# A dilated gated convolution on one core: four buffers for chunks and sums, loads issued earlier, and new places for the side work

## The chip, the cores and the metric

The kernel runs on one core of a Trainium2 chip. The core has a matrix engine (TensorE, PE in the profile; its weight loads are PEld), a vector engine (VectorE, DVE), an engine for activations and copies (ScalarE, ACT), a general engine (GpSimd, POOL) and an engine that here only issues DMAs (SyncE, SP). On-chip data lie in SBUF, results of matmuls in PSUM, inputs and outputs in device memory. The metric is the device time of one execution, in microseconds (us).

## The reference

The input `x` has 2 sequences of 16000 steps with 256 channels, `w` holds three taps of 256 x 512, `w_o` is 256 x 256, all in bf16. With a dilation of 2 and causal padding:

```
h[t] = x[t] @ w[0] + x[t-2] @ w[1] + x[t-4] @ w[2]     # steps before the first are 0
f, g = h[..., :256], h[..., 256:]
out = (tanh(f) * sigmoid(g)) @ w_o
```

So each step needs three products of depth 256 and width 512, a gate, and one product of depth 256 and width 256.

## The kernel before

**Rows, chunks, groups.** Four consecutive steps of a sequence form one row, so a sequence has 4000 rows. A row's steps are the four phases j of a tile `xt`, which a transposing DMA fills with channels on the partitions. A *plain group* is up to 256 rows (1024 steps). A *chunk* is what one load brings, usually two groups (`load_chunk`, L135). Plain groups don't multiply three taps: from xc, yp (the two phase pairs, one of them a row earlier) DVE makes the difference `m` (`pre_m`, L316) and the sum `p` (`pre_p`, L322), POOL makes the differences `d` (`pre_d`, L328), and four products with sums of the taps' weights (`products`, L345) replace six. For each group `oi` runs over the four output blocks of 128 channels.

**p in two ways.** For the first groups DVE computes `p`. For chunks from `P_DMA` on it is a tile `ps`: a second transposing DMA loads half of it (`load_sums`, L151), and a DMA issued by POOL adds the other half in place (`add_sums`, L159), at a slot set by `ACC_LAG`.

**Wide groups.** Four groups of each sequence are taken with eight steps to a row. A wide group (`load_wide`, L210) gets its operands `qa`, `qb`, `qd` by POOL (`wide_part`, L219, six parts), `qp` by DVE for the first and POOL for the others (`wide_sum`, L244) and `qm` by DVE (`wide_diff`, L254). Its output blocks take 14 matmuls of 256 columns each instead of eight of 512. They need further sums of the weights, made in twelve steps of two halves (`weight_step`, L614; places in `W_AT`, engine in `W_ENG`), and the first wide group's parts at the places of `P_AT`, its sum and difference at `SUM_AT` and `DIFF_AT`.

**Order.** The program is written in one order, and each engine keeps it. The list `slots` (L544) holds 104 plain slots (group, oi) and 32 wide ones, placed by `SPACING`: so many plain slots, then a wide one. The loop at L645 handles slot k: the first products of slot k, the second products of slot k-1 (which need DVE's `combine` of slot k-1, L390), at most one output piece (`out_mm`, L448; none at slots in `HOLD`, two in `TWICE`), DVE's combine, and then side work: gates (`gate`, L424), `pre_m`, weight steps, POOL's parts, accumulations, ACT's activations, loads. A piece's result goes from PSUM to `osb` in the next slot, by ACT or in some cases by DVE (`EVICT_DVE`), and SP stores two pieces at a time. `osb` has four buffers.

**POOL behind DVE.** `after` (L308) makes a POOL operation wait for DVE's last operation on SBUF operands in its slot, so that POOL reads SBUF while DVE's sums read PSUM.

**Loads.** SP issues all chunk, sum and wide loads and nearly all stores, in order. Chunk tiles `xt` and sums `ps` have three buffers each, wide tiles `xq` two. A chunk is loaded in the last slot of a group when the next group lies in a chunk two before it (L762). Wide group n + 2 is loaded in the last slot (oi = 3) of wide group n (L711).

Of the kernel before, what the change touches and what calls it, by code (L numbers as in the profile page):

```python
# [9 lines left out]
ALU = mybir.AluOpType  # L10
# [3 lines left out]
def kernel(  # L14
# [19 lines left out]
    nc = tc.nc  # L34
    bf16 = mybir.dt.bfloat16
    f32 = mybir.dt.float32
    B, T, D = x.shape
    K, _, D2 = w.shape
    P = 128
    assert K == 3 and D % P == 0 and D2 == 2 * D and T % 64 == 0  # L40
    CT = D // P
    NT = D // P
    RH = 16
    RG = 256
# [4 lines left out]
    LAST = ((128,), (128, 128))  # L49
    N_DIRECT = 4  # L50
    N_WIDE = (4, 4)
    SPACING = (31, 1, 3, 1, 4, 2, 2, 2, 3, 1, 2, 2, 2, 1, 1, 1, 2, 1, 1, 2, 2, 1, 2, 1, 2, 1, 1, 2, 2, 1, 1, 2,)
    W_ENG = (0, 0, 0, 0, 0, 0, 0, 1, 0, 0, 0, 0)
    W_AT = (7, 7, 11, 14, 14, 14, 17, 17, 19, 19, 22, 25, 26, 27, 29, 29, 29, 30, 30, 30, 33, 34, 36, 36)
    P_AT = (9, 10, 10, 11, 12, 13, 14, 15, 16, 16, 17, 19, 20, 20, 21, 22, 24, 24, 25, 25, 26, 27, 29, 29)
    SUM_AT, DIFF_AT = 21, 25
    HOLD = (23,)
    TWICE = (113,)
    COPIES = 0
    EVICT_DVE = ()  # L60
    SUM_POOL = True
    SHORT_LAST = True
    GATE2 = False
    P_DMA = 4
    ACC_LAG = (6, 6, 6, 6, 7, 9, 13, 7, 6, 6, 6, 11, 9, 7, 10, 8, 13, 14, 8, 10)
    Q_PARTS = ((0, 1), ("s", 2), (3, 4), (5,))
    SPLIT_PROJ = 1
    W_STEP = 2
# [10 lines left out]
    groups, chunks, wides = [], [], []  # L79
    starts = [0] * B  # L80

    def add_groups(b, rs, cuts=()):
        cuts, i = list(cuts), 0
        while i < len(rs):
            n = cuts.pop(0) if cuts else 2
            part = rs[i:i + n]
            chunks.append((b, starts[b], sum(part), len(groups), len(part)))
            for r in part:
                col = starts[b] - chunks[-1][1]
                groups.append(dict(wide=False, b=b, r0=starts[b], R=r, chunk=len(chunks) - 1, col=col))  # L90
                starts[b] += r
            i += n

    ends = []
    for b in range(B):
        wide = N_WIDE[min(b, 1)]
# [11 lines left out]
    XW = max(c[2] for c in chunks)  # L108

    consts = ctx.enter_context(tc.tile_pool(name="consts", bufs=1))  # L110
    xt_pool = ctx.enter_context(tc.tile_pool(name="xt", bufs=3))
    d_pool = ctx.enter_context(tc.tile_pool(name="dd", bufs=3))
    p_pool = ctx.enter_context(tc.tile_pool(name="pp", bufs=3))
    ps_pool = ctx.enter_context(tc.tile_pool(name="ps", bufs=3))
    m_pool = ctx.enter_context(tc.tile_pool(name="mm", bufs=3))
    ss_pool = ctx.enter_context(tc.tile_pool(name="ss", bufs=3))
    xq_pool = ctx.enter_context(tc.tile_pool(name="xq", bufs=2))
# [4 lines left out]
    osb_pool = ctx.enter_context(tc.tile_pool(name="osb", bufs=4))  # L122
# [10 lines left out]
    xts = {}  # L133

    def load_chunk(c):  # L135
        b, r0, rc, _, _ = chunks[c]
        xt = xt_pool.tile([P, 4, CT, RH + XW], bf16, name="xt")
        xts[c] = xt
        if r0 == 0:
            nc.gpsimd.memset(xt[:, :, :, RH - 1:RH], 0.0)  # L140
        if c == 0:
            return
        lo = 0 if r0 == 0 else RH
        nc.sync.dma_start_transpose(
            out=xt[:, :, :, RH - lo:RH + rc].rearrange("p j ct r -> p (j ct) r"),
            in_=x[b, 4 * (r0 - lo):4 * (r0 + rc), :].rearrange("(r j) c -> r (j c)", j=4),
        )

    def load_sums(c):  # L151
        b, r0, rc, _, _ = chunks[c]
        sums[c] = ps_pool.tile([P, 2, CT, XW], bf16, name="ps")
        nc.sync.dma_start_transpose(
            out=sums[c][:, :, :, :rc].rearrange("p j ct r -> p (j ct) r"),
            in_=x[b, 4 * r0:4 * (r0 + rc), :].rearrange("(r j) c -> r (j c)", j=4)[:, :2 * D],
        )

    def add_sums(c):  # L159
        rc = chunks[c][2]  # L160
        nc.gpsimd.dma_start(
            out=sums[c][:, :, :, :rc], in_=xts[c][:, 2:4, :, RH - 1:RH - 1 + rc], accum_op=ALU.add,
        )
        added.add(c)

    sums, added = {}, set()
# [1 line left out]
    nc.vector.memset(warm[:], 0.0)  # L168
    w_taps = [consts.tile([P, CT, D2], bf16, name=f"w{k}_sb") for k in range(K)]
    wo_sb = consts.tile([P, NT, D], bf16)  # L170
    xn = consts.tile([P, 4, D], bf16, name="xn")
    w_in = [w[k].rearrange("(ct c) d -> c ct d", c=P) for k in range(K)]
    nc.sync.dma_start(out=xn[:], in_=x[0, 0:4 * P, :].rearrange("(r j) c -> r j c", j=4))
    for k in (TAPS[0], TAPS[2]):
# [6 lines left out]
    for c in range(2):  # L181
        load_chunk(c)
    load_chunk(2)
    loaded = 3

    wd0_sb = consts.tile([P, CT, D2], bf16)
    wd2_sb = consts.tile([P, CT, D2], bf16)
    ws_sb = consts.tile([P, CT, D2], f32)
    wf_sb = consts.tile([P, CT, D2], f32)
    wu_sb = consts.tile([P, CT, D2], bf16)  # L190
    wt_sb = consts.tile([P, CT, D2], bf16)
    wp_sb = consts.tile([P, CT, D2], bf16)
# [129 lines left out]
    def pre_p(g):  # L322
        xp, yp, xc, yc = views(g)
        G = groups[g]
        G["p"] = p_pool.tile([P, 2, CT, RG], bf16, name="pp")
        return nc.vector.tensor_tensor(out=G["p"][:, :, :, :G["R"]], in0=xc, in1=yp, op=ALU.add)

    def pre_d(g, part, eng, behind=None):  # L328
        xp, yp, xc, yc = views(g)
# [9 lines left out]
        return ins  # L339

    def sum_view(G, ct):
        assert G["chunk"] in added
        return sums[G["chunk"]][:, :, ct, G["col"]:G["col"] + G["R"]]

    def products(k, which):  # L345
        G, oi = at(k)
        o = O_ORDER[oi]
        osl = slice(o * P, (o + 1) * P)
        R = G["R"]
        N = 2 * R  # L350
        if which in (1, 2):
            G["ab"[which - 1], oi] = (ps_a, ps_b)[which - 1].tile([P, 2 * RG], f32, name="ab"[which - 1])
        wmat, mv, bank, first = {
            2: (wm_sb, lambda ct: G["m"][:, :, ct, :R], "b", True),
            1: (wp_sb, lambda ct: sum_view(G, ct) if G["chunk"] >= P_DMA else G["p"][:, :, ct, :R], "a", True),
            3: (wd0_sb, lambda ct: G["d"][:, 2:4, ct, :R], "b", False),
            0: (wd2_sb, lambda ct: G["d"][:, 0:2, ct, :R], "a", False),
        }[which]
        for ct in range(CT):
            nc.tensor.matmul(  # L360
                G[bank, oi][:, :N], lhsT=wmat[:, ct, osl], rhs=mv(ct),
                start=first and ct == 0, stop=ct == CT - 1, skip_group_check=True,
            )
# [178 lines left out]
    NG = len(groups)  # L542
# [3 lines left out]
    for i, (_, g, oi) in enumerate(plain):  # L546
        slots.append(plain[i])
        since += 1
        full = all(groups[plain[j][1]]["R"] == RG for j in range(max(i - 2, 0), min(i + 2, len(plain))))
        if rest and since >= SPACING[4 * len(wides) - len(rest)] and full:  # L550
            slots.append(rest.pop(0))
            since = 0
    assert not rest
    NB = len(slots)
# [55 lines left out]

    for i, kk in enumerate(W_AT):
        extra.setdefault(kk, []).append((i // 2, i % 2))
# [17 lines left out]

    load_wide(0)
    wides_loaded = 1
    unadded = []
    wide_parts = {}
    for i, kk in enumerate(P_AT):
        wide_parts.setdefault(kk, []).append((i // 4, i % 4))
# [7 lines left out]
    k = N_DIRECT + 1  # L644
    while k <= NB:  # L645
        w, g, oi = slots[k] if k < NB else END
        G = None if k == NB else at(k)[0]
# [41 lines left out]
        if w:  # L689
            if oi == 2 and not GATE2:  # L690
                last = gate(G, 0)
            elif oi == 0 and g > 0:
                last = gates(wides[g - 1])
                drain(wides[g - 1], k + 2)
            elif oi == 1 and g + 1 < len(wides) and not SUM_POOL:
                last = wide_sum(g + 1)
            elif oi == 3 and g + 1 < len(wides):
                last = wide_diff(g + 1)
            for step in held:
                step(last)  # L700
            held = []
            if g + 1 < len(wides):
                for part in Q_PARTS[oi]:
                    if part == "s":
                        wide_sum(g + 1, last or filled)
                    else:
                        wide_part(g + 1, part, last or filled)
            wide_sums(G, oi)
            wide_combine(G, oi)
            activate(k - 1)  # L710
            if oi == 3 and wides_loaded < len(wides):  # L711
                load_wide(wides_loaded)
                wides_loaded += 1
            k += 1
            continue
# [4 lines left out]
            pre_d(g, 3, nc.vector)  # L720
        if k < NB and oi == (1 if g == 1 else 0) and g + 1 < NG:
            last = pre_m(g + 1)
        elif k < NB and oi == 2 and g + 1 < NG and groups[g + 1]["chunk"] < P_DMA:
            last = pre_p(g + 1)
        elif oi == 3 and g < NG and (not GATE2 or g == NG - 1):
            last = gate(G, 0)
        elif oi == 1 and 1 < g < NG:
            last = gates(groups[g - 1])
            drain(groups[g - 1], k + 2 if g < NG - 1 else k + 1)
# [29 lines left out]
                    wide_part(0, part, last, slice(i // 2, i // 2 + 1), slice(i % 2, i % 2 + 1))  # L759
        if k < NB:  # L760
            activate(k - 1)
        if k < NB and oi == 3 and loaded < len(chunks) and groups[min(g + 1, NG - 1)]["chunk"] + 2 >= loaded:  # L762
            load_chunk(loaded)
            load_sums(loaded)
            unadded.append((loaded, k + ACC_LAG[loaded]))
            loaded += 1
            if wides_loaded == 1:
                load_wide(1)
                wides_loaded = 2
# [33 lines left out]
```

## Time and profile before

| | |
|---|---|
| median of 3 runs | 281.22 us (280.15 to 282.76) |
| the profiled execution | 282.09 us |
| its span | 280.3 us |
| busy in the span: PE, DVE, ACT, POOL | 273.7, 257.8, 261.4, 172.8 us |
| granted clock of PE | 1.0 throughout |
| data moved by DMA | 45.34 MB, mean 162 GB/s |

The span runs from the first to the last instruction of the profiled execution; the rest of its time lies around it. A row of a group gives line, engine, operation, tiles written and read, shapes, count, then busy time and the mean of one in ns, then idle time of the engine before them and what ended it. A row of a timeline gives start, length, engine (with q for the queue that issues DMAs), line, operation, tiles, shapes, and in brackets idle time and its end. L numbers are lines of the kernel before.

### The profile page before, as it was taken

Reading aid. Unit: us, or ns where it says so; the run is one execution under the profiler, and the core shown is the slowest. Engines: PE = TensorE matmul, PEld = TensorE weight load, DVE = VectorE, ACT = ScalarE, POOL = GpSimd, SP = SyncE. Lnnn points to the kernel's source line nnn. Section 1 sums busy time; section 2 is a strip of 40 time slices with the busy share of each in tenths; the row PEclk is TensorE's granted clock in tenths of the full one; section 3 lists DMA queues with packets and bytes.
Section 4 is the critical chain, followed back from the end, with each engine's and each line's share of the span. In section 5 each row is a group of like instructions: output and inputs, shape, how many; then the busy total and the mean of one; then the engine's idle time right before and its main releaser. Section 6 shows DMA issues by size and latency. Waiting matters only on the chain.

```text
span 280.3 us, 5448 instructions
## 1 busy us (share of the span) xinstructions
PE 273.7 (98%) x1818; PEld 177.7 (63%) x1818; DVE 257.8 (92%) x471; ACT 261.4 (93%) x564; POOL 172.8 (62%) x186
## 2 busy tenths in 40 slices
PE   8999999999999999999899999999999999999995
PEld 6645555446665666666556767666767667678783
DVE  3999999999999989998999999999999999897884
ACT  5798999989999999999799999999999999999995
POOL 1148978787785876546967647677649643224630
PEclk9999999999999999999999999999999999999999
DMA  8999999962786998997966297269564924253423
GB/s 218 217 224 261 216 213 208 236 118 75 185 190 137 188 203 190 123 235 199 265 139 137 89 209 205 83 134 201 159 129 93 187 87 88 78 136 114 94 88 123
DMA packets 105340, 45.34 MB, mean 162 GB/s; under 512 B 89952, under 2 KB 97504, under 8 KB 105312
## 3 DMA queue, kind: packets, MB, share of 16 engines
q1 hardware_dynamic: 98016, 39.10, 60.8%
q0 software_dynamic: 6336, 5.18, 13.9%
q10 hardware_dynamic: 960, 0.72, 0.8%
q8 instruction: 14, 0.23, 0.3%
q14 instruction: 14, 0.11, 0.1%
HBM read 1.18 MB, written 16.38 MB: 63 GB/s over the span
## 4 chain that ended last, share of the span: by engine, by line
PE 94%; DVE 4%; issue 1%; DVEq 0%
PE b L360 27%; PE a L360 27%; PE o_ps L459 18%; PE a L263 13%; PE b L263 5%; PE a L131 1%; PE a L378 1%; PE b L378 1%; DVE b L394 1%; DVE zw L435 1%; DVE b L298 1%; DVE qm L258 1%; DVE a L395 0%; PE tp L200 0%; DVE zz L435 0%
## 5 line engine op out<-in xcount | busy, mean ns | idle before, releaser
L337 POOL TENSOR_TENSOR dd<-xt 128x512 bf16<-128x512 bf16 (+2 forms) x95 | 93.8, 995 | 79.7 <-DVE zz L435 36.2
L394 DVE TENSOR_TENSOR b<-a,ss 128x512 f32<-128x512 f32 (+2 forms) x100 | 64.8, 648 | 6.9 <-ACT ss L388 3.9
L395 DVE TENSOR_TENSOR a<-a,ss 128x512 f32<-128x512 f32 (+2 forms) x100 | 64.2, 642 | 0.0
L388 ACT COPY ss<-b 128x512 f32<-128x512 f32 (+2 forms) x100 | 57.8, 578 | 6.1 <-PE b L360 2.0
L360 PEld LDWEIGHTS <-wd_sb 128*128 128x128 bf16 x400 | 38.8, 98 | 35.1 <-issue 3.1
L459 PE MATMUL o_ps<-wo_sb,zz 128*128 128x256 bf16 x360 | 60.7, 273 | 0.0
L360 PE MATMUL b<-dd,wd_sb 128*128 128x512 bf16 (+2 forms) x200 | 55.6, 360 | 0.7 <-DVE b L394 0.7
L360 PE MATMUL a<-dd,wd_sb 128*128 128x512 bf16 (+2 forms) x200 | 55.6, 360 | 0.0
L360 PE MATMUL b<-mm,wm_sb 128*128 128x512 bf16 (+2 forms) x200 | 55.6, 360 | 0.0
L496 ACT CAST osb<-o_ps 128x512 bf16<-128x512 f32 x87 | 53.4, 614 | 0.0
L459 PEld LDWEIGHTS <-zz 128*128 128x128 bf16 x360 | 35.2, 98 | 20.8
L360 PE MATMUL a<-ps,wp_sb 128*128 128x512 bf16 (+2 forms) x160 | 43.8, 355 | 0.0
L435 DVE TENSOR_TENSOR zz<-th,sg 128x1024 bf16<-128x1024 bf16 (+1 forms) x51 | 33.4, 656 | 0.0
L418 ACT ACTIVATE th<-b 128x512 bf16<-128x512 f32 (+2 forms) x52 | 31.1, 598 | 2.1 <-PE b L360 1.1
L360 PEld LDWEIGHTS <-wp_sb 128*128 128x128 bf16 x200 | 19.6, 98 | 19.8
L418 ACT ACTIVATE sg<-b 128x512 bf16<-128x512 f32 (+2 forms) x52 | 31.1, 597 | 0.9 <-PE b L360 0.6
L418 ACT ACTIVATE th<-a 128x512 bf16<-128x512 f32 (+2 forms) x52 | 31.2, 600 | 0.0
L418 ACT ACTIVATE sg<-a 128x512 bf16<-128x512 f32 (+2 forms) x52 | 31.2, 600 | 0.0
L298 DVE TENSOR_TENSOR b<-ud,a 128x512 f32<-128x512 f32 x32 | 22.3, 696 | 6.4 <-PE a L263 4.1
L233 POOL TENSOR_TENSOR qa<-xq 128x512 bf16<-128x512 bf16 (+2 forms) x21 | 22.9, 1090 | 4.5 <-DMA xq<-in_x_dram 4.5
L288 DVE SCALAR_TENSOR_TENSOR ud<-b,sw 128x256 f32<-128x256 f32 x64 | 24.0, 417 | 0.2 <-ACT sw L281 0.2
L459 PE MATMUL o_ps<-wo_sb,zw 128*128 128x256 bf16 x128 | 22.8, 273 | 0.0
(77 smaller groups left out, 433.1 us busy)
## 6 DMA issues: line engine op xcount, KB each, us to landing
out_dram<-osb SPq DMA_DIRECT2D x60, 256.0 KB, 2.5
ps<-xt POOLq DMA_DIRECT2D x8, 512.0 KB, 6.6
ps<-xt POOLq DMA_DIRECT2D x2, 288.0 KB, 4.9
w_sb<-in_w_dram ACTq DMA_DIRECT2D x2, 256.0 KB, 4.2
out_dram<-osb_end SPq DMA_DIRECT2D x3, 128.0 KB, 1.7
xn<-in_x_dram SPq DMA_DIRECT2D x1, 256.0 KB, 3.0
w_sb<-in_w_dram SPq DMA_DIRECT2D x1, 256.0 KB, 4.1
ps<-xt POOLq DMA_DIRECT2D x1, 256.0 KB, 5.2
```

The source lines that it names most:

```text
L263: nc.tensor.matmul(G[bank, oi][:, half * RG:(half + 1) * RG], lhsT=wmat[:, ct, o * P:(o + 1) * P], rhs=mv[:, :, ct, :], start=first and ct ...
L288: nc.vector.scalar_tensor_tensor(out=G["ud", oi][:, h], in0=G["b", oi][:, RG:], scalar=0.5, in1=G["ss", oi][:], op0=ALU.mult, op1=op)
L298: nc.vector.tensor_tensor(out=G["b", oi][:], in0=ud, in1=G["a", oi][:], op=ALU.subtract)
L337: ins = eng.tensor_tensor(out=G["d"][:, j, :, :R], in0=a[:, q], in1=s[:, q], op=ALU.subtract)
L360: nc.tensor.matmul(G[bank, oi][:, :N], lhsT=wmat[:, ct, osl], rhs=mv(ct), start=first and ct == 0, stop=ct == CT - 1, skip_group_check=True,)
L388: nc.scalar.copy(out=G["ss", oi][:, :N], in_=G["b", oi][:, :N])
L394: nc.vector.tensor_tensor(out=pb[:, :N], in0=pa[:, :N], in1=ss[:, :N], op=ALU.subtract)
L395: nc.vector.tensor_tensor(out=pa[:, :N], in0=pa[:, :N], in1=ss[:, :N], op=ALU.add)
L418: nc.scalar.activation(out=dst[:, 2 * h:2 * h + 2, :R], in_=G[bank, oi][:, :2 * R].rearrange("p (q r) -> p q r", q=2), func=func, scale=1. ...
L435: return nc.vector.tensor_tensor(out=G["z"][:, dt, :, :full], in0=G["th"][:, dt, :, :full], in1=G["sg"][:, dt, :, :full], op=ALU.mult)
L459: nc.tensor.matmul(o_ps[:, q, :], lhsT=lhsT, rhs=wo_sb[:, dt, :], start=(dt == 0), stop=(dt == NT - 1),)
L496: copy(out=osb[:, 2 * jp:2 * jp + 2, :], in_=o_ps[:])
```

## The change

- `xt` and `ps` get four buffers (`XT_BUFS`, `PS_BUFS`). Room comes from three places: `p` made by DVE now goes into `ps` tiles, the weight difference `wf_sb` shares the tile of `ws_sb`, and the first input tile `xn` takes an `osb` buffer.
- `P_DMA` counts groups now: DVE makes `p` for groups 1 to 4, and the DMA from group 5 on. Chunk 3 (groups 4 and 5) gets its first half by DVE and its second by DMA (`plain_rows`).
- A wide group is loaded at oi = 0 of the wide group two before it (`LOAD_OI`), instead of oi = 3. Chunks from number 6 on (`MORE_FROM`) are loaded one chunk earlier. `INIT` stays 3, so its branch for 4 isn't taken.
- The tables of places are new: `SPACING`, `W_ENG`, `W_AT`, `P_AT`, `SUM_AT`, `HOLD`, `TWICE`, `EVICT_DVE`, `ACC_LAG`.

```diff
-    SPACING = (31, 1, 3, 1, 4, 2, 2, 2, 3, 1, 2, 2, 2, 1, 1, 1, 2, 1, 1, 2, 2, 1, 2, 1, 2, 1, 1, 2, 2, 1, 1, 2,)
-    W_ENG = (0, 0, 0, 0, 0, 0, 0, 1, 0, 0, 0, 0)
-    W_AT = (7, 7, 11, 14, 14, 14, 17, 17, 19, 19, 22, 25, 26, 27, 29, 29, 29, 30, 30, 30, 33, 34, 36, 36)
-    P_AT = (9, 10, 10, 11, 12, 13, 14, 15, 16, 16, 17, 19, 20, 20, 21, 22, 24, 24, 25, 25, 26, 27, 29, 29)
-    SUM_AT, DIFF_AT = 21, 25
-    HOLD = (23,)
-    TWICE = (113,)
+    SPACING = (30, 1, 4, 1, 4, 2, 1, 2, 3, 2, 2, 2, 1, 1, 2, 1, 2, 1, 2, 2, 1, 1, 2, 1, 2, 1, 1, 3, 1, 1, 1, 2,)
+    W_ENG = (0, 0, 0, 0, 0, 0, 0, 0, 0, 0, 1, 0)
+    W_AT = (5, 7, 14, 15, 16, 16, 17, 17, 19, 19, 22, 22, 23, 25, 27, 27, 28, 29, 30, 30, 31, 31, 32, 33)
+    P_AT = (9, 11, 11, 12, 13, 14, 15, 16, 16, 18, 19, 19, 20, 21, 22, 22, 24, 24, 25, 26, 27, 27, 28, 28)
+    SUM_AT, DIFF_AT = 20, 25
+    HOLD = ()
+    TWICE = (103,)
...
-    EVICT_DVE = ()
+    EVICT_DVE = (81,)
...
-    P_DMA = 4
-    ACC_LAG = (6, 6, 6, 6, 7, 9, 13, 7, 6, 6, 6, 11, 9, 7, 10, 8, 13, 14, 8, 10)
+    P_DMA = 5
+    LOAD_OI = 0
+    MORE_FROM = 6
+    XT_BUFS, PS_BUFS, AHEAD, INIT = 4, 4, 2, 3
+    ACC_LAG = (6, 6, 6, 5, 7, 9, 16, 14, 9, 16, 12, 19, 6, 7, 10, 7, 13, 9, 7, 15)
...
-    xt_pool = ctx.enter_context(tc.tile_pool(name="xt", bufs=3))
+    xt_pool = ctx.enter_context(tc.tile_pool(name="xt", bufs=XT_BUFS))
...
-    p_pool = ctx.enter_context(tc.tile_pool(name="pp", bufs=3))
-    ps_pool = ctx.enter_context(tc.tile_pool(name="ps", bufs=3))
+    ps_pool = ctx.enter_context(tc.tile_pool(name="ps", bufs=PS_BUFS))
...
+    def plain_rows(c):
+        return sum(groups[g]["R"] for g in range(chunks[c][3], P_DMA))
...
     def load_sums(c):
         b, r0, rc, _, _ = chunks[c]
+        lo = plain_rows(c)
         sums[c] = ps_pool.tile([P, 2, CT, XW], bf16, name="ps")
         nc.sync.dma_start_transpose(
-            out=sums[c][:, :, :, :rc].rearrange("p j ct r -> p (j ct) r"),
-            in_=x[b, 4 * r0:4 * (r0 + rc), :].rearrange("(r j) c -> r (j c)", j=4)[:, :2 * D],
+            out=sums[c][:, :, :, lo:rc].rearrange("p j ct r -> p (j ct) r"),
+            in_=x[b, 4 * (r0 + lo):4 * (r0 + rc), :].rearrange("(r j) c -> r (j c)", j=4)[:, :2 * D],
         )
...
     def add_sums(c):
-        rc = chunks[c][2]
+        rc, lo = chunks[c][2], plain_rows(c)
         nc.gpsimd.dma_start(
-            out=sums[c][:, :, :, :rc], in_=xts[c][:, 2:4, :, RH - 1:RH - 1 + rc], accum_op=ALU.add,
+            out=sums[c][:, :, :, lo:rc], in_=xts[c][:, 2:4, :, RH - 1 + lo:RH - 1 + rc], accum_op=ALU.add,
         )
...
-    xn = consts.tile([P, 4, D], bf16, name="xn")
+    xn = osb_pool.tile([P, 4, D], bf16, name="osb")
...
-    wf_sb = consts.tile([P, CT, D2], f32)
+    wf_sb = ws_sb
...
-        G["p"] = p_pool.tile([P, 2, CT, RG], bf16, name="pp")
-        return nc.vector.tensor_tensor(out=G["p"][:, :, :, :G["R"]], in0=xc, in1=yp, op=ALU.add)
+        if G["chunk"] not in sums:
+            sums[G["chunk"]] = ps_pool.tile([P, 2, CT, XW], bf16, name="ps")
+        return nc.vector.tensor_tensor(out=sums[G["chunk"]][:, :, :, G["col"]:G["col"] + G["R"]], in0=xc, in1=yp, op=ALU.add)
...
-            1: (wp_sb, lambda ct: sum_view(G, ct) if G["chunk"] >= P_DMA else G["p"][:, :, ct, :R], "a", True),
+            1: (wp_sb, lambda ct: sum_view(G, ct), "a", True),
...
-            if oi == 3 and wides_loaded < len(wides):
+            if oi == LOAD_OI and wides_loaded < len(wides):
...
-        elif k < NB and oi == 2 and g + 1 < NG and groups[g + 1]["chunk"] < P_DMA:
+        elif k < NB and oi == 2 and g + 1 < NG and g + 1 < P_DMA:
...
-        if k < NB and oi == 3 and loaded < len(chunks) and groups[min(g + 1, NG - 1)]["chunk"] + 2 >= loaded:
+        if k < NB and oi == 3 and loaded < len(chunks) and groups[min(g + 1, NG - 1)]["chunk"] + AHEAD + (loaded >= MORE_FROM) >= loaded:
```

More of the change, by code (lines that the diff above doesn't have):

```diff
@@ L89, in add_groups @@
                 col = starts[b] - chunks[-1][1]
-                groups.append(dict(wide=False, b=b, r0=starts[b], R=r, chunk=len(chunks) - 1, col=col))
+                groups.append(dict(wide=False, g=len(groups), b=b, r0=starts[b], R=r, chunk=len(chunks) - 1, col=col))
                 starts[b] += r
@@ L183 @@
     load_chunk(2)
-    loaded = 3
+    if INIT == 4:
+        load_chunk(3)
+        load_sums(3)
+    loaded = INIT
     wd0_sb = consts.tile([P, CT, D2], bf16)
@@ L341, in sum_view @@
     def sum_view(G, ct):
-        assert G["chunk"] in added
+        assert G["g"] < P_DMA or G["chunk"] in added
         return sums[G["chunk"]][:, :, ct, G["col"]:G["col"] + G["R"]]
@@ L632 @@
     wides_loaded = 1
-    unadded = []
+    unadded = [(3, 7 + ACC_LAG[3])] if INIT == 4 else []
     wide_parts = {}
```

## The prediction

> **What bounds the kernel now.** I read the page first, then the waits, then the timeline around each wait of TensorE (PE). From the page, the chain that ended last, by engine:
>
> ```profile
> PE 94%; DVE 4%; issue 1%; DVEq 0%
> ```
>
> PE is the bound: 94% of the chain that sets the end is its matmuls, and the change leaves their number and shapes alone. So only the stretches in which PE waited can be won. The longest wait of PE on another engine in the view of waits (total, times, longest):
>
> ```profile
> PE b L263 <- DVE b L298: 1.3, 1, 1.3
> ```
>
> That understates the loss, since the modelled matmuls overlap. Slots show it better: the loop handles one slot k after another, and a slot's first product is a `b<-mm` (plain) or `a<-qp` (wide). Around this wait, these starts on PE (start, length):
>
> ```profile
> 120.94 0.38 PE L263 MATMUL a<-qp,wm_sb 128*128 128x256 bf16 x2
> 123.34 0.59 PE L360 MATMUL b<-mm,wm_sb 128*128 128x512 bf16 x2
> 125.07 0.38 PE L263 MATMUL a<-qp,wm_sb 128*128 128x256 bf16 x2
> ...
> 133.76 0.59 PE L360 MATMUL b<-mm,wm_sb 128*128 128x512 bf16 x2
> 137.14 0.59 PE L360 MATMUL b<-mm,wm_sb 128*128 128x512 bf16 x2
> 139.31 0.38 PE L263 MATMUL a<-qp,wm_sb 128*128 128x256 bf16 x2
> 141.84 0.59 PE L360 MATMUL b<-mm,wm_sb 128*128 128x512 bf16 x2
> 144.02 0.59 PE L360 MATMUL b<-mm,wm_sb 128*128 128x512 bf16 x2
> ```
>
> Undisturbed, a plain slot behind a wide one takes 125.07 − 123.34 = 1.73 us and a wide one 123.34 − 120.94 = 2.40. The plain slot at 133.76 took 3.38 (1.65 too long), the wide one at 139.31 took 2.53 (0.13), the plain one at 141.84 took 2.18 (0.45). **Loss 1: 2.23 us.** Its cause, from the timeline of all engines:
>
> ```profile
> 111.41 7.11 SPq L154 DMA_TRANSPOSE ps<-in_x_dram  x1
> 119.67 3.45 SPq L214 DMA_TRANSPOSE xq<-in_x_dram  x1
> 125.79 0.68 DVE L435 TENSOR_TENSOR zz<-th,sg 128x1024 bf16<-128x1024 bf16 x1
> 128.41 1.16 POOL L233 TENSOR_TENSOR qa<-xq 128x512 bf16<-128x512 bf16 x1 [4.52 <-DMA xq<-in_x_dram]
> 131.88 1.37 DVE L435 TENSOR_TENSOR zz<-th,sg 128x1024 bf16<-128x1024 bf16 x1
> 132.66 1.61 POOL L233 TENSOR_TENSOR qa<-xq 128x512 bf16<-128x512 bf16 x1
> 133.17 1.64 DVE L435 TENSOR_TENSOR zw<-thw,sgw 128x1024 bf16<-128x1024 bf16 x1
> 137.98 1.30 DVE L320 TENSOR_TENSOR mm<-xt 128x1024 bf16<-128x1024 bf16 x1
> ```
>
> SP, which issues loads and stores in order, was in a transpose of sums until 118.5 and issued the fourth wide group's load only at 119.67; it reached POOL at 128.4. POOL, 4.5 us late, then ran beside VectorE's (DVE's) operations on two SBUF operands, which its dependencies (`behind`) otherwise keep apart; they took 1.37, 1.64 and 1.30 instead of the 0.68 of the row at 125.79 (all three have that size). Those 2.27 us of DVE came out on PE as loss 1.
>
> Earlier, where the weights of the wide groups are made, PE's slots and three rows of DVE and POOL:
>
> ```profile
> 48.96 0.59 PE L360 MATMUL b<-mm,wm_sb 128*128 128x512 bf16 x2
> 51.02 0.59 PE L360 MATMUL b<-mm,wm_sb 128*128 128x512 bf16 x2
> ...
> 55.34 0.59 PE L360 MATMUL b<-mm,wm_sb 128*128 128x512 bf16 x2
> 55.94 1.29 POOL L161 DMA_DIRECT2D ps<-xt  x1
> 56.51 1.41 DVE L258 TENSOR_TENSOR qm<-qa,qb 128x1024 bf16<-128x1024 bf16 x1
> 56.76 1.61 POOL L233 TENSOR_TENSOR qd<-xq 128x256 bf16<-128x256 bf16 x1
> 57.51 0.59 PE L360 MATMUL b<-mm,wm_sb 128*128 128x512 bf16 x2
> 60.65 0.59 PE L360 MATMUL b<-mm,wm_sb 128*128 128x512 bf16 x2
> ...
> 77.69 0.59 PE L360 MATMUL b<-mm,wm_sb 128*128 128x512 bf16 x2
> 79.42 0.38 PE L263 MATMUL a<-qp,wm_sb 128*128 128x256 bf16 x2
> ```
>
> A plain slot with an output piece takes 57.51 − 55.34 = 2.17, one without 79.42 − 77.69 = 1.73. Slot 23 (48.96, without a piece: HOLD) took 2.06: **loss 2, 0.33.** Slot 27 (57.51) took 3.14: **loss 3, 0.97**, where `qm` met a `qd` that the DMA issue at 55.94 had pushed back.
>
> **The change part by part.**
>
> *Wide loads at the first slot of a wide group instead of the last* (LOAD_OI). The fourth wide group's load moves from the slot that began at 112.49 to the one at 93.61:
>
> ```profile
> 93.61 0.38 PE L263 MATMUL a<-qp,wm_sb 128*128 128x256 bf16 x2
> ...
> 112.49 0.38 PE L263 MATMUL a<-qp,wm_sb 128*128 128x256 bf16 x2
> ```
>
> It then stands on SP right behind the two transposes of a chunk load in slot 43, which begins some 2.2 us before 93.61. Even if both took as long as the 7.1 us of the row at 111.41, SP would reach the wide load near 106, and with the 8.7 us from its issue to POOL's start seen above (119.67 to 128.41) it is there near 115, before the next wide group, now one slot ahead of 120.94. POOL's wait goes, and with it loss 1: **−2.23**, between −2.23 and 0 if POOL is late there anyway. What is next there is PE itself. The buffer overwritten is the current wide group's; its last reader, part 5, was queued on POOL in the wide slot before, so SP waits little; behind SP stand stores, which four output buffers (two pieces each, eight slots) cover.
>
> *Four buffers, chunks from the seventh one chunk earlier.* No engine but POOL waits for loads now, so this alone is worth 0. The same transposes are issued, in other company. In this view of 95 to 103 us (packets, MB, share of the engines) the accumulating queue q0 shares with SP's q1, in that of 134 to 140 us q1 is nearly alone:
>
> ```profile
> DMA packets 3480, 1.27 MB, mean 159 GB/s; under 512 B 2968, under 2 KB 3480, under 8 KB 3480
> q1 hardware_dynamic: 2952, 0.75, 80.3%
> q0 software_dynamic: 528, 0.52, 55.9%
> ...
> DMA packets 5760, 1.68 MB, mean 281 GB/s; under 512 B 5636, under 2 KB 5636, under 8 KB 5759
> ```
>
> Together they moved 159 GB/s, alone 281. The new ACC_LAG still puts accumulations beside loads (slots 42, 60), so SP will be held at places again; but every load then has ten slots or more (some 20 us) to its products, and five or more to its accumulation. 0.
>
> *p by DMA from group 5.* DVE loses one `pp`, and chunk 3's sums, which were already loaded and accumulated whole though unused, are now handled for half their rows (as in the second row, the median of one to landing):
>
> ```profile
> L326 DVE TENSOR_TENSOR pp<-xt 128x1024 bf16<-128x1024 bf16 x5 | 3.7, 742 | 0.0
> ps<-xt POOLq DMA_DIRECT2D x1, 256.0 KB, 5.2
> ```
>
> −0.74 us of DVE at slot 18, in a stretch where it is never idle. The DVE writes one half of that tile and the DMA the other; no wait between them, as ACT and DVE show, which write interleaved parts of one `xt` at the same time:
>
> ```profile
> 4.48 0.80 ACT L202 COPY xt<-tp 128x256 bf16<-128x256 bf16 x2 [1.44 <-PE tp L200]
> 4.69 0.72 DVE L202 COPY xt<-tp 128x256 bf16<-128x256 bf16 x2 [3.69 <-PE tp L200]
> ```
>
> Were that wrong, DVE would stand up to 5.2 us at slot 14 and PE nearly as long; I give it almost no chance.
>
> *New places of weights, parts, sums; HOLD and TWICE.* DVE has 15 weight instructions before and after, and POOL one. `qp` moves from slot 21 to 20, so DVE's pair before loss 2 shrinks by one operation, after 0.74 less at slot 18; and slot 23 gets its piece, 0.43 us more of PE for DVE to catch up in. Nine weight instructions of DVE instead of seven fall before slot 25. I take loss 2 as gone, **−0.3** (between −0.33 and 0). Slot 25 keeps what made loss 3: the same accumulation at slot 24, the same half `qd` behind it, `qm` at 25. What DVE saves before is used up by the two weight instructions that move ahead: **0** (between −0.97 and +0.3, the second by one stretched half step). HOLD's empty slot becomes slot 35, which TWICE doesn't change in sum. Ten of the 32 wide slots move by one place; wide and plain slots alternated as densely before: 0.
>
> *One eviction on DVE* at slot 81, a plain slot with the half gate: ACT saves an operation and DVE, reading PSUM as in its combine, gains one. One operation is taken up in the plain slots behind the wide one that follows: 0 (up to +0.3).
>
> *Accumulations moved on POOL.* Each takes POOL 1.29 us. They now come at slots 60 and 63, amid the third wide group, and at 80 and 81, amid the fifth; before only single ones lay near. The window behind the disturbed stretch shows POOL's room in some four slots:
>
> ```profile
> 146.00:154.00 8.00, 8.00 (x59) 5.38 (x57) 7.36 (x15) 7.72 (x18) 5.09 (x6) 1.00 0.64 132
> ```
>
> (Pairs of busy time and count for PE, its weight loads, DVE, ACT and POOL.) POOL is busy 5.09 us of 8.00 and 2.9 free; two accumulations take 2.6 of that. The one at 55.94 led to loss 3, most others to nothing: **+0.3** for both (between 0 and 4.5).
>
> Sum: −2.23 − 0.3 + 0.3 = **−2.2 us**. Against the profiled execution's 282.09 us (span 280.3, 1.8 around it) that gives 279.9. The median of the runs, 281.22, lies 0.87 lower: if ordinary runs pay the same stalls, they end at 279.0; if the 0.87 is stall that they don't pay, at 279.9. I take **279.3**, between the two.
>
> **The rivals.**
>
> *More is won:* loss 3 goes too, because DVE and POOL reach slot 24 in another phase, and DVE saves the two weight steps that now come before slot 34. 279.0 − 0.97 = 278.0, and at the best, with the small remaining waits, 277. For: DVE has less to do ahead of it. Against: the order at slots 24 and 25 is the same.
>
> *The stall only moves:* POOL is late in the third wide group without the wait, through the two accumulations. Then only loss 2 goes: 280.9. For: 2 × 1.29 us added within four slots (8 us). Against: 2.6 still fits in the free 2.9, and the wait was 4.5.
>
> *Slower:* paired accumulations make POOL late by more than its free time in both wide groups, and each costs what loss 1 did, 2.23: 279.0 + 4.5 = 283.5; with the three accumulations at slots 35, 38 and 42 acting alike, 285.7. It decides from the point where POOL is late by more than its free 2.9 us in four slots; the pairs bring 2.6. On the page "SBUF — State Buffer", section "Who interferes with whom", the Trainium skill says that a DVE operation with two SBUF inputs and a GpSimd one that reads SBUF lock each other out for the whole instruction. By that rule, three meetings with an operation of 1.04 us would cost DVE 3.1 us, the trace has 2.27; with 3.1 the rival ends at 285.2 instead.
>
> *It doesn't do what it says:* the wide loads land no earlier, since SP is held by chunk loads. 281 to 281.5. Against: 19 us of lead, and at most 15 of them lost.
>
> **How the numbers follow.** Forecast as summed (278.0 to 280.6): 0.46. More won (below that): 0.28. Stall moves or no effect (280.6 to 282): 0.08. Slower (282 and above): 0.18, two thirds of it above 284. About 1% is what a measurement of this kernel can tell from no change; 1% of 281.22 is 2.8, so faster is below 278.4 and slower above 284.0. Faster: 0.28 and 0.07 of the forecast's lower edge, 0.35. Slower: 0.12. Same: 0.53. The range leaves out the better case's tail (0.06) and what lies above two harmed wide groups (0.14): 277.1 to 283.3.
>
> **What would show it.** The waits no longer have POOL's 4.5 us for xq; the DVE rows of `zz`, `zw` and `mm` in the third wide group are near 0.69; plain slots there take 1.73 and 2.17 again; slot 23 takes 2.17 with a piece; slot 27 still takes about 3.1. Wrong would be: POOL without idle time at slots 60 to 65 or 80 to 85 with `zz`, `zw` or `mm` over 1.2, or ACT waiting for output buffers while SP stands in a transpose.

## The result, and the profile after

The changed kernel takes **279.63 us** in the median of 22 runs (279.29 to 280.98), the kernel before beside it 281.52 (22 runs, 279.73 to 285.11). Runs more than 1.5% above the fastest of the same kernel count as slow and are left out of the ratios and of every value of the kernel before from here on: here that is one run, and without it the kernel before has 281.34 (279.73 to 283.86). The ratio is 0.9938, with a 95% interval of 0.9917 to 0.9958: a gain of 0.6%. The fastest runs of the two are only 0.44 us apart, the medians 1.7, the slowest 2.9: as if the change took away a delay that the kernel before pays in varying amount. The profiled execution took 279.56 (span 277.8), 2.53 less than that of before.

From the page, the chain that ended last, by engine:

```profile
PE 95%; DVE 3%; issue 1%; ACT 1%; DVEq 0%
```

PE still sets the end, and DVE's part fell from 4% to 3%. The view of waits, PE's longest wait on DVE behind the start-up (total, times, longest):

```profile
PE b L370 <- DVE b L404: 0.3, 1, 0.3
```

PE's 1.3 us on DVE are gone, and so are POOL's 4.52 for `xq`: the view has no wait for `xq` any more. The same places as in the prediction, on PE:

```profile
133.96 0.59 PE L370 MATMUL b<-mm,wm_sb 128*128 128x512 bf16 x2
135.69 0.59 PE L370 MATMUL b<-mm,wm_sb 128*128 128x512 bf16 x2
137.86 0.38 PE L272 MATMUL a<-qp,wm_sb 128*128 128x256 bf16 x2
140.25 0.59 PE L370 MATMUL b<-mm,wm_sb 128*128 128x512 bf16 x2
```

The plain slot at 133.96 (slot 63) takes 1.73 instead of 3.38, the wide one at 137.86 takes 2.39 instead of 2.53. DVE's operations there, and the load in front of them on SP:

```profile
95.12 5.11 SPq L160 DMA_TRANSPOSE ps<-in_x_dram  x1
100.33 2.19 SPq L223 DMA_TRANSPOSE xq<-in_x_dram  x1
...
132.08 0.68 DVE L445 TENSOR_TENSOR zz<-th,sg 128x1024 bf16<-128x1024 bf16 x1
132.68 0.68 DVE L445 TENSOR_TENSOR zw<-thw,sgw 128x1024 bf16<-128x1024 bf16 x1
136.53 0.69 DVE L329 TENSOR_TENSOR mm<-xt 128x1024 bf16<-128x1024 bf16 x1
```

SP was held by a slow sums transpose again (5.11), as the prediction allowed; but the wide load behind it left at 100.33 instead of 119.67, and `zz`, `zw` and `mm` take 0.68, 0.68 and 0.69.

Where the difference lies along the program: the first products of slots 43, 66, 75 and 103, at which both kernels have done the same number of plain and wide slots, in the kernel before (slot 66 is the prediction's row at 141.84):

```profile
91.45 0.59 PE L360 MATMUL b<-mm,wm_sb 128*128 128x512 bf16 x2
...
161.35 0.59 PE L360 MATMUL b<-mm,wm_sb 128*128 128x512 bf16 x2
...
219.45 0.59 PE L360 MATMUL b<-mm,wm_sb 128*128 128x512 bf16 x2
```

and in the changed one (slot 66 is the row at 140.25 above):

```profile
91.65 0.59 PE L370 MATMUL b<-mm,wm_sb 128*128 128x512 bf16 x2
...
158.93 0.59 PE L370 MATMUL b<-mm,wm_sb 128*128 128x512 bf16 x2
...
216.97 0.59 PE L370 MATMUL b<-mm,wm_sb 128*128 128x512 bf16 x2
```

The changed kernel is 0.20 us *later* at slot 43, 1.59 earlier at 66, 2.42 at 75, 2.48 at 103. So in these two executions all of the gain, 2.6 us, is made between slots 43 and 75, nothing behind them, and a little is lost before.

### The profile page after: what moved, and what is told of

Its sections match the earlier page's. It is cut to its first block, busy times and chain, and to the rows that moved or that the text cites. A ratio compares the mean times of both kernels' runs of the same rounds, so it can differ in the third digit from the quotient of the medians.

```text
span 277.8 us, 5452 instructions
## 1 busy us (share of the span) xinstructions
PE 272.7 (98%) x1818; PEld 177.4 (64%) x1818; DVE 255.6 (92%) x471; ACT 260.0 (94%) x563; POOL 172.6 (62%) x186
## 4 chain that ended last, share of the span: by engine, by line
PE 95%; DVE 3%; issue 1%; ACT 1%; DVEq 0%
PE a L370 28%; PE b L370 28%; PE o_ps L469 19%; PE a L272 12%; PE b L272 5%; PE a L133 1%; PE a L388 1%; PE b L388 1%; DVE b L404 1%; DVE a L405 0%; ACT ss L398 0%; DVE qm L267 0%; DVE b L307 0%; DVE ws_sb L635 0%; DVE ud L297 0%
## 5 line engine op out<-in xcount | busy, mean ns | idle before, releaser
L347 POOL TENSOR_TENSOR dd<-xt 128x512 bf16<-128x512 bf16 (+2 forms) x95 | 92.6, 978 | 83.9 <-DVE zz L445 32.5
L370 PE MATMUL a<-ps,wp_sb 128*128 128x512 bf16 (+2 forms) x200 | 55.7, 360 | 0.0
L308 DVE TENSOR_TENSOR a<-ud,a 128x512 f32<-128x512 f32 x32 | 22.1, 690 | 0.0
```

Of the source, the lines that this page charges most:

```text
L347: ins = eng.tensor_tensor(out=G["d"][:, j, :, :R], in0=a[:, q], in1=s[:, q], op=ALU.subtract)
L370: nc.tensor.matmul(G[bank, oi][:, :N], lhsT=wmat[:, ct, osl], rhs=mv(ct), start=first and ct == 0, stop=ct == CT - 1, skip_group_check=True,)
```

## The experiments

The theory: an accumulation running beside transposes holds SP, the fourth wide load comes late, POOL falls upon DVE, PE waits; to take that away is the gain. Rivals: the gain comes from the new places, from the earlier chunks, or from DVE's spared `p`. No run changes the number of buffers alone. Each ratio below is to the kernel before on the same chip; medians of different chips are compared with care.

**Is it the late load?** First, in the kernel before, one number: the lag of chunk 8's accumulation goes from 6 to 10 slots. It comes at slot 54 instead of 49 (slot 53 is a wide one), out of the way of the transposes of chunk 9.

```diff
-    ACC_LAG = (6, 6, 6, 6, 7, 9, 13, 7, 6, 6, 6, 11, ...
+    ACC_LAG = (6, 6, 6, 6, 7, 9, 13, 7, 10, 6, 6, 11, ...
```

> The kernel before with one number changed: the accumulation of chunk 8 four slots later (ACC_LAG[8] from 6 to 10), so that it no longer runs beside the load of chunk 9. Theory (an accumulation beside transposes holds SP and makes the fourth wide load late): the sums' transpose at 111 us takes near 2 instead of 7.1 us, SP issues the wide load at 113 to 116 instead of 119.7, POOL waits under 1.5 us, and the time falls by 0.5 to 1.5 us. Rival (SP is held by PE, whose products release the buffer): the transpose still ends near 118 and nothing is gained.

Measured: 280.01 us (279.63 to 280.56; before 280.48, 279.60 to 283.57), ratio 0.9972 (0.9940 to 1.0005). In the kernel before, the timeline has the accumulation at

```profile
106.77 1.29 POOL L161 DMA_DIRECT2D ps<-xt  x1 [1.33 <-PE o_ps L459]
```

and with the changed number, on SP and POOL:

```profile
106.47 4.71 SPq L144 DMA_TRANSPOSE xt<-in_x_dram  x1
111.28 1.67 SPq L154 DMA_TRANSPOSE ps<-in_x_dram  x1
...
114.89 2.34 SPq L214 DMA_TRANSPOSE xq<-in_x_dram  x1
...
117.39 1.27 POOL L161 DMA_DIRECT2D ps<-xt  x1
```

The sums transpose takes 1.67 instead of 7.11 and ends at 113, so the rival (PE holds SP) is out. The wide load leaves 4.8 us earlier, and it takes 4.8 us from issue to landing instead of 8.6: it no longer runs beside chunk 9's accumulation, which POOL issued at 121.52 before and at 121.10 now, behind the landing. So the load came late for two reasons, SP's delay and its own slow transfer. POOL doesn't wait, `zz`, `zw` and `mm` take 0.68 or 0.69, and PE loses nothing in the third wide group; the profiled execution is 2.0 us shorter (280.05 and 282.09). The ratio's gain is 0.28%, some 0.8 us, and its interval just includes 1, because the runs of the kernel before lie 4.0 us apart; those with the changed number lie within 0.9. So the trace and the narrow spread carry the verdict that the chain of causes is as stated; how much of the median it explains is not settled by them.

Next, only the slot of the wide loads, all of them or the fourth alone, in the kernel before:

```diff
-            if oi == 3 and wides_loaded < len(wides):
+            if oi == 0 and wides_loaded < len(wides):                                # all
+            if oi == (0 if wides_loaded == 3 else 3) and wides_loaded < len(wides):  # fourth alone
```

> The kernel before with nothing changed but the slot of the wide loads (oi = 0 instead of 3). Theory (the late load of the fourth wide group is the whole gain): 1.5 to 2.3 us faster than the kernel before, near 279.6, and no wait of POOL for xq; the slots at 133.8 to 144 us take 1.73, 2.17 and 1.73 again. Rival (the gain is that of the four buffers, or of the new places): within 0.5 us of the kernel before. Rival (SP is held by the chunk load in front, so the wide load lands no earlier): POOL still waits for xq.

> The kernel before with only one of the eight wide loads moved, that of the fourth wide group (oi = 0 instead of 3). Theory: the same gain as with all moved, to 0.4 us, since POOL waited for this one alone. Rival (earlier wide loads help everywhere, by thinning the transfers behind them): less than half of that gain.

Measured: all of them, 281.05 (before 281.49), ratio 0.9972 (0.9937 to 1.0008); the fourth alone, 280.26, ratio 0.9990 (0.9955 to 1.0025). With all moved, SP, POOL and DVE:

```profile
95.67 7.86 SPq L154 DMA_TRANSPOSE ps<-in_x_dram  x1
103.62 3.31 SPq L214 DMA_TRANSPOSE xq<-in_x_dram  x1
...
108.63 9.44 SPq L144 DMA_TRANSPOSE xt<-in_x_dram  x1
...
107.65 1.29 POOL L161 DMA_DIRECT2D ps<-xt  x1 [1.91 <-PE b L263]
111.47 1.12 DVE L320 TENSOR_TENSOR mm<-xt 128x1024 bf16<-128x1024 bf16 x1
```

POOL's wait for `xq` is gone, but less is won than was expected: the accumulations stand where they stood, one of them makes the next chunk transpose 9.44 us long, and their issue still pushes POOL onto DVE (`mm` 1.12), which costs PE 0.4 and 0.6 us at two places. With the fourth load alone, the profiled run has no loss in the third wide group, but of 12 runs nine lie at 279.7 to 280.6 and three at 282.3 to 283.0. No trace shows one of the three, so why they are late stays open. Neither interval is clear of 1: by time alone neither run shows a gain.

**Is the early wide load needed in the new kernel?** The changed kernel with the old slot of the wide loads:

```diff
-    LOAD_OI = 0
+    LOAD_OI = 3
```

> The changed kernel with the wide loads back at oi = 3. Theory: SP has no slow chunk load in front of the fourth wide load there (the last ended at 113.4 and no accumulation is beside the load), so it is issued near 113.5 and lands near 119 to 121, as POOL comes to it: a wait under 1 us and less than 0.6 us lost against the changed kernel. Rival (the early wide load itself is what gains): 1.5 us or more lost, near 281.3, with a wait of POOL for xq of some us.

Measured: 287.03 (285.95 to 288.19; before 281.49), ratio 1.0204 (1.0156 to 1.0252): slower than both kernels, where the theory had expected a small loss and the rival a clear one. It isn't the fourth wide load that is late, but the fifth. The timeline:

```profile
132.18 7.60 SPq L146 DMA_TRANSPOSE xt<-in_x_dram  x1
...
146.71 3.54 SPq L223 DMA_TRANSPOSE xq<-in_x_dram  x1
...
152.85 1.15 POOL L242 TENSOR_TENSOR qa<-xq 128x512 bf16<-128x512 bf16 x1 [7.68 <-DMA xq<-in_x_dram]
...
156.98 1.01 PE L370 MATMUL a<-dd,wd_sb 128*128 128x512 bf16 x2 [4.89 <-POOL dd L347]
```

The same mechanism stands at another place, with a higher price: POOL waits 7.68 us, this time ahead of a difference that PE itself needs (4.89). In the changed kernel that load leaves at 118.99, ahead of the slow transposes. So the new arrangement needs the early load.

**Places or loads?** The new tables without the new loads, buffers and `p` (in the kernel before), and the opposite, the changed kernel with the old tables:

```diff
     # before, with the new SPACING, W_ENG, W_AT, P_AT, SUM_AT, HOLD, TWICE, EVICT_DVE
     # after, with the old ones of the same names; ACC_LAG as it was in each
```

> The kernel before with the new places alone (SPACING, W_ENG, W_AT, P_AT, SUM_AT, HOLD, TWICE, EVICT_DVE); loads, buffers, p and accumulation lags as before. Theory: the fourth wide group's load is late as before, so little is gained: 280.5 to 282.3, with POOL's wait for xq. Rival (the new places bring the gain): near 279.6.

> The changed kernel with the places of before (SPACING, W_ENG, W_AT, P_AT, SUM_AT, HOLD, TWICE, EVICT_DVE); buffers, loads, p and ACC_LAG as changed. Theory now (early loads, chunks and wide groups together, keep transfers from coming late, and the places don't matter for that): 279.0 to 280.0, no wait of POOL for xq, its runs within 1.5 us of each other. Rival (the gain needs the new places too): 280.5 or more.

Measured: new tables alone 282.82 (before 281.49), ratio 1.0056 (1.0022 to 1.0091), 0.6% slower; the rest of the change alone 280.14 (279.75 to 280.74; before 280.48), ratio 0.9966 (0.9929 to 1.0003). The first is slower than theory and rival had it. In it POOL still waits for `xq`, three times and 3.0 us in all, and on DVE:

```profile
151.84 2.83 DVE L320 TENSOR_TENSOR mm<-xt 128x1024 bf16<-128x1024 bf16 x1
```

One `mm` takes 2.83 instead of 0.69, and PE then waits 1.35 us on DVE. In the second, no engine waits for `xq`, the runs lie within 1.0 us, and PE loses 0.5 to 0.7 at three places (34.6, 58.6, 97.1 us). So by the ratios the loads, buffers and `p` give about half (0.34% of 0.62%) and the new places the rest, but only with early loads. The intervals overlap, and that of the second run just includes 1, so the split is only indicated.

**The chunks one earlier.** The changed kernel without the lead, first with its lags as they are, then with lags set so that each accumulation comes in good time for its group:

```diff
-    MORE_FROM = 6
+    MORE_FROM = 99
-    ACC_LAG = (6, 6, 6, 5, 7, 9, 16, 14, 9, 16, 12, 19, ...    # second kernel only
+    ACC_LAG = (6, 6, 6, 5, 7, 9, 12, 4, 6, 10, 6, 5, ...
```

> The changed kernel with chunks loaded two ahead throughout (MORE_FROM out of reach), so that only the chunk loads move back. Theory now: chunk loads, wide loads and accumulations crowd again in the third wide group, POOL comes late and 0.7 to 2.5 us are lost against the changed kernel (280.3 to 282.1). Rival (nobody waited for a chunk, so its lead is worth nothing): 279.6 to within 0.4 us.

> The changed kernel with chunks loaded two ahead throughout, and the accumulation lags set so that each accumulation comes at the changed kernel's slot where the chunk is there by then, and about six slots behind its load otherwise (slots 35, 38, 50, 60, 68, 80 for chunks 6 to 11). Theory now (what the chunk lead gives is room to place the accumulations away from loads; by itself it is worth little): 279.6 to 280.6, and no PE wait for sums. Rival (the lead itself is needed, as the run with the lags unchanged seemed to say): above 281.5.

Measured: 284.54 (before 280.48), ratio 1.0141 (1.0086 to 1.0196), and 279.65 (before 280.75), ratio 0.9957 (0.9932 to 0.9982). The first is slower than its theory and its rival had it. In it PE waits for sums:

```profile
99.77 0.86 PE L370 MATMUL a<-ps,wp_sb 128*128 128x512 bf16 x2 [3.34 <-DMA ps<-xt]
```

A lag counts slots from the load, so a load moved back takes its accumulation with it. Chunk 6's came at slot 40 instead of 35, and slot 45 needs it; POOL issued it at 90.47, beside chunk 8's transposes, and it took 9.3 us to land. The transfers crowd, as the theory says, but the lags bring them together: the run tested the lags, not the lead. With fitting lags the kernel without the lead has the changed one's time (279.65 and 279.63, on different chips; ratios 0.9957 and 0.9938, with overlapping intervals): no gain of the lead alone is seen.

**p by DMA for group 5.** The changed kernel with DVE making `p` for groups 4 and 5, chunk 3 without sums by DMA:

```diff
-    P_DMA = 5
+    P_DMA = 6
...
+        if lo == rc:
+            return
```

> The changed kernel with the sum p of group 5 made by DVE at slot 18, as before, and no transposed or accumulated sums for chunk 3. Prediction's step: DVE pays 0.7 us where it is never idle, PE up to 0.4 us of it (279.6 to 280.1). Rival (DVE has room for it): 279.6 to within 0.15 us, or less, since one accumulation on POOL is gone as well.

Measured: 279.81 (279.33 to 280.35; before 280.75), ratio 0.9950 (0.9924 to 0.9975), within 0.2 us of the changed kernel. DVE's `p` for group 5 comes back on PE as a loss of 0.5 in slot 22, and without chunk 3's accumulation (next part) 0.36 is saved ahead of it, in slots 18 and 19.

**What is left before slot 43.** In the changed kernel, chunk 3's accumulation now comes at slot 12, and the one at slot 24 stays (POOL and DVE):

```profile
30.06 1.41 POOL L167 DMA_DIRECT2D ps<-xt  x1
32.10 1.40 DVE L336 TENSOR_TENSOR ps<-xt 128x1024 bf16<-128x1024 bf16 x1
...
56.23 1.29 POOL L167 DMA_DIRECT2D ps<-xt  x1
56.91 1.29 DVE L267 TENSOR_TENSOR qm<-qa,qb 128x1024 bf16<-128x1024 bf16 x1
57.05 1.61 POOL L242 TENSOR_TENSOR qd<-xq 128x256 bf16<-128x256 bf16 x1
```

Each time the 1.3 or 1.4 us of the issue makes POOL's next operations meet DVE's (`p` 1.40, `qm` 1.29 instead of 0.7). Three kernels move these apart: both accumulations later; chunk 3's later and `qm` a slot later; and that with the last four weight steps moved from slots 28 to 33 to slots 31 to 36.

```diff
-    ACC_LAG = (6, 6, 6, 5, 7, 9, ...
+    ACC_LAG = (6, 6, 6, 6, 7, 12, ...    # first
+    ACC_LAG = (6, 6, 6, 6, 7, 9, ...     # second and third
-    SUM_AT, DIFF_AT = 20, 25
+    SUM_AT, DIFF_AT = 20, 26             # second and third
-    W_AT = (..., 27, 27, 28, 29, 30, 30, 31, 31, 32, 33)
+    W_AT = (..., 27, 27, 33, 33, 31, 31, 34, 34, 36, 36)    # third
```

> The changed kernel with two accumulations moved: that of chunk 3 from slot 12 to 13 (as before), that of chunk 5 from slot 24 to 27. Theory (a DMA issue of 1.3 us on POOL pushes the next POOL operations onto DVE's): the sum of group 4 takes near 0.7 instead of 1.40 us, qm near 0.7 instead of 1.29, slot 27 takes 2.2 to 2.5 instead of 2.8, and the time falls by 0.4 to 0.9 us against the changed kernel, to 278.8 to 279.2. Rival (the collision moves on to the next DVE operation): within 0.3 us of the changed kernel.

> The changed kernel with qm of the first wide group one slot later (DIFF_AT 26, a slot in which DVE has its combine alone) and the accumulation of chunk 3 at slot 13 as before. Theory (loss 3 is DVE's load in slot 25, gate, qm and a weight step in one slot, together with POOL's lateness): slot 27 takes 2.2 to 2.5 instead of 2.8 us, slots 4 to 24 lose 0.2 to 0.4 us less, the time falls to 278.7 to 279.3. Rival (what is saved is lost a few slots on, as with the accumulation of chunk 5 moved): 279.4 to 279.8.

> The kernel with qm at slot 26 and the accumulation of chunk 3 at slot 13, and in addition the last weight steps moved behind the first two wide slots (steps 8 to 11 at slots 33, 31, 34 and 36 instead of 28 to 33). Theory (what qm's move saved was partly lost again because DVE came late to the first wide slot): the slot of W0.0 takes 2.4 instead of 2.66 us and the next plain one 1.9 to 2.0 instead of 2.19, and the time falls by 0.2 to 0.5 us against that kernel, to 278.7 to 279.1. Rival (the loss moves on to slots 33 to 40): within 0.2 us of 279.24.

Measured: 279.56 (before 280.48), ratio 0.9963 (0.9930 to 0.9996); 279.24 (279.06 to 279.56; before 280.75), ratio 0.9936 (0.9912 to 0.9960); 279.17 (278.38 to 280.75; before 280.67), ratio 0.9947 (0.9916 to 0.9979). In the first, `p` takes 0.86 and `qm` 0.68, but the moved accumulation meets the next pair (POOL, DVE):

```profile
62.49 1.29 POOL L167 DMA_DIRECT2D ps<-xt  x1
...
65.19 1.45 DVE L445 TENSOR_TENSOR zz<-th,sg 128x1024 bf16<-128x1024 bf16 x1
```

and PE's slot behind it takes 2.54 instead of 1.73, 0.8 too long (1.90 in the changed kernel): the collision moved on. In the second, the slots on PE:

```profile
57.67 0.60 PE L370 MATMUL b<-mm,wm_sb 128*128 128x512 bf16 x2
59.84 0.59 PE L370 MATMUL b<-mm,wm_sb 128*128 128x512 bf16 x2
...
64.17 0.38 PE L272 MATMUL a<-qp,wm_sb 128*128 128x256 bf16 x2
66.83 0.59 PE L370 MATMUL b<-mm,wm_sb 128*128 128x512 bf16 x2
```

Slot 27 takes 2.17 (2.80 in the changed kernel, 3.14 before) and begins at 57.67, against 58.14; the wide slot at 64.17 (W0.0, the first of the first wide group) takes 2.66, some 0.3 too long, and the plain one behind it 2.19 instead of 1.90. So from slot 27 to slot 33 the second kernel takes 13.75 us against 13.82 in the changed one: most of what `qm`'s move saved is lost a few slots on, as its rival has it, though the time came out as the theory says. In the third that slot takes 2.47:

```profile
64.33 0.38 PE L272 MATMUL a<-qp,wm_sb 128*128 128x256 bf16 x2
66.80 0.59 PE L370 MATMUL b<-mm,wm_sb 128*128 128x512 bf16 x2
```

but its median is only 0.07 below the second's. The loss moved on, as the rival has it: slot 37 takes 2.78 (2.51 in the second) and slot 38 takes 1.90 (1.74). The medians of the last two lie some 0.4 us below the changed kernel's 279.63, but on other chips, and their ratios (0.9936 and 0.9947) are no better than its 0.9938: whether they beat it stays open.

## Why the prediction was right, point by point

The time came to 279.63 against a forecast of 279.3, by the mechanism that carried most of the sum. That the rest of the sum came out so close is luck, since three errors nearly cancel in the profiled executions: ahead of slot 43, 0.2 us were lost where 0.3 were to be won; the paired accumulations cost nothing instead of 0.3; and 0.4 us were won where the sum has no term.

- **Loss 1 (−2.23): right.** Between slots 43 and 66 the profiled executions differ by 0.20 + 1.59 = 1.79; its third part, slot 66 of before (0.45, now 1.74 long instead of 2.18), follows behind that point. The step "late load, POOL late, DVE stretched, PE waits" was shown by chunk 8's accumulation moved alone; that the load's own transfer was slow as well (8.6 us) is inside the 8.7 us that the prediction took from the rows, but it named only SP's delay as the cause. SP was held at the new place, as foreseen, and 19 us of lead covered it. Another 0.4 us was won at slots 69 and 73 (1.92 and 1.95 long before, 1.74 now), which the sum didn't list. With the old places slot 69 takes 1.74 as well and slot 73 still 1.94; their causes stay open.
- **Loss 2 (−0.3): right at its slot, wrong in sum.** Slot 23 now takes 2.16 with its piece, as the rows show (starts on PE):

```profile
49.49 0.59 PE L370 MATMUL b<-mm,wm_sb 128*128 128x512 bf16 x2
51.65 0.60 PE L370 MATMUL b<-mm,wm_sb 128*128 128x512 bf16 x2
```

  But it begins 0.53 later than before (48.96). The step that failed is "Accumulations moved on POOL", which went through slots 60, 63, 80 and 81 and left out chunk 3's, now at slot 12: it stretches `p`, and PE loses 0.36 in slots 18 and 19 (38.3 to 43.0), where before lost 0.07. With that accumulation a slot later, `p` takes 0.86, and these 0.36 shrink to 0.11. Another 0.35 (0.10 before) is lost at 11.6 to 12.8, ahead of that accumulation. It belongs to this one execution: kernels with the same code up to there lose 0.04 or less (no lead and fitting lags; late wide loads). So of the 0.47 us by which slot 27 begins earlier with `qm` moved, 0.31 are there already at slot 9. The cause of that early loss stays open.
- **Loss 3 (0, between −0.97 and +0.3):** slot 27 took 2.80 instead of 3.14, −0.34. The collision foreseen is there, a little smaller.
- **Paired accumulations (+0.3): mis-sized, they cost next to nothing.** In the changed kernel two stand together in the fifth wide group, and the DVE row behind them is the only one touched:

```profile
172.79 2.58 POOL L167 DMA_DIRECT2D ps<-xt  x2
...
178.23 0.78 DVE L329 TENSOR_TENSOR mm<-xt 128x1024 bf16<-128x1024 bf16 x1
```

  `mm` took 0.78 instead of 0.69, and at slots 60 to 66 nothing was lost. That fits the argument against the rival "slower", that the free 2.9 us take up their 2.6. That rival's 3.1 us for three meetings counts whole POOL operations of 1.04; in the rows DVE starts partway into one (`mm` at 137.98, POOL's `qd` from 137.69 to 138.73) and lost 0.62, less than the 0.75 that was left of it. That rival had a real mechanism, though: with the late wide load the changed kernel is 2.0% slower. Its condition, POOL late by more than its free time, was met there by a load, not by two accumulations.
- **Chunks earlier, p by DMA: 0 and next to 0, right as far as these runs can tell.** Without the lead and with fitting lags 279.65; with DVE's `p` 279.81, both on another chip.
- **The offset between profiled execution and median.** The kernel before varies by 4.1 us from run to run, the kernel with chunk 8's accumulation moved by 0.9, the changed one by 1.7: so the 0.87 that its median lay below the profiled execution was probably in part stall that other runs don't pay, and the median's gain (1.7) is smaller than the profile's (2.53). 279.63 lies between the two ends of the prediction, 279.0 and 279.9, nearer the upper. For the profiled execution the sum gave 279.9, and 279.56 came; the three errors named first make up the difference.

## What to carry to other kernels

When an engine waits for a load, look at what the issuing queue stood in before it: here a transpose ahead of it was slowed from 1.7 to 7.1 us by an accumulation on another queue, and the load itself, beside the next accumulation, took 8.6 us to land where the other wide loads took 4.5 to 6.9. One number that moved the first accumulation brought the median to within 0.4 us of the whole change (280.01 and 279.63, on different chips; by the ratios 0.28% of 0.62%). A place counted from a load (a lag) moves when the load moves, so set both together. In these runs a side engine that fell behind cost time in two ways: where its next operation met one of the vector engine (`mm` 1.30 instead of 0.69), and where the matrix engine needed its result (4.89 us). Shifting such a meeting by a few slots moved it on, in whole or in part, in all three kernels that tried it ahead of slot 43.

## What the hardware showed that was not expected

After the two longest pauses of PE in these runs, the matmuls behind them ran at half rate. In the changed kernel with late wide loads, windows around its pause (busy time and count for PE, its weight loads, DVE, ACT, POOL; then granted clock, DMA share, GB/s):

```profile
146.00:152.00 6.00, 6.00 (x43) 3.97 (x41) 5.70 (x11) 5.97 (x14) 0.00 (x0) 1.00 1.21 256
152.00:158.00 6.00, 1.11 (x5) 0.40 (x4) 3.96 (x5) 1.06 (x3) 5.15 (x5) 0.89 0.34 127
158.00:164.00 6.00, 6.00 (x39) 4.18 (x38) 3.02 (x6) 4.45 (x10) 5.16 (x6) 0.82 0.00 0
164.00:170.00 6.00, 6.00 (x41) 3.84 (x40) 5.62 (x11) 5.97 (x14) 2.93 (x3) 1.00 0.91 205
```

The granted clock falls to 0.89 and 0.82 and is back at 1.00 behind 164. The pair of 512 columns at 156.98, quoted above, is 1.01 long instead of 0.59; a pair of 256 is 0.63 and later 0.38 again:

```profile
158.64 0.63 PE L272 MATMUL a<-qp,wm_sb 128*128 128x256 bf16 x2
...
160.88 0.38 PE L469 MATMUL o_ps<-wo_sb,zw 128*128 128x256 bf16 x2
```

From 156.98 to about 160.4 matmuls ran at half rate, so the wait of 4.9 us cost about half of these 3.4 us, 1.7, once more: together 6.6, which is what slots 71 and 72 of this kernel took longer than those of the changed one (11.13 and 4.55 us). Behind the wait of 3.34 us for sums matmuls were long as well (0.86 at 99.77), with a granted clock of 0.50 from 100 to 103 us. This agrees with the Trainium skill, "TensorE: Matmul & The Clock Gate", section "Part 1: The HAM clock gate": the clock halves after an idle window of about 3.4 us and comes back after a busy one. In the kernels before and after no wait of PE in the loop is that long, and their granted clock is 1.0.

An accumulation beside transposes was known from the trace of before to lower the rate (159 GB/s together, 281 for transposes alone). That one such meeting also bears on how far the runs of a kernel lie apart was not expected: with one accumulation moved, the spread shrank from 4.0 us to 0.9. That the wide load comes late to a different degree in each run would explain it; that is not shown, since the kernel before has one trace.
